# A fused linear-attention and gated-convolution kernel: a list scheduler in place of a hand-made order, with cheaper matmul work

## The chip, the cores and the metric

The kernel runs on one core of one Trainium2 chip. The metric is the device time of one execution in microseconds (us). A "span" is the time from the first to the last instruction in the profile; the time is 1.7 to 3.1 us longer in all runs with both on record.

The engines, as the profile calls them: PE is the matmul engine (PEld are its weight loads), DVE is VectorE, ACT is ScalarE, POOL is GpSimd, SP is SyncE, which here only issues DMAs. Each engine takes its own work in the order of the program: in the trace of the changed kernel, the 69 operations of POOL, 104 of DVE and 183 of ACT that could be matched by name all ran in the planned order.

## The reference, cut to what matters

The first stage is a recurrent attention over 4 batches x 8 heads x 768 steps x 48 channels; the second is a projection, a circular convolution through an FFT, a gate and an output projection on 4 x 768 x 384.

```python
for t in range(S):                                   # stage 1, per batch and head
    cur = einsum('bhd,bhe->bhde', u * k_t, v_t)
    y[:, :, t] = einsum('bhd,bhde->bhe', r_t, state + cur)
    state = w_t[..., None] * state + einsum('bhd,bhe->bhde', k_t, v_t)
# stage 2, x = y with heads joined
x1, x2, x3 = split(x @ w_proj, 3)
x2_conv = irfft(rfft(x2) * rfft(filter), n=S)        # along the sequence
out = (x1 * x2_conv * x3) @ w_out
```

Both kernels cut the sequence into chunks of 128 steps, so there are 24 chunks, 6 to a batch. In a chunk, cumulative sums of log(w) turn the recurrence into a masked 128 x 128 product of scaled q and k for each head, plus one product with the state. The FFT is a set of matmuls with a cosine/sine table `F`; the inverse uses its transpose `m2`.

## The kernel before: the parts that the change touches

The kernel before emits its instructions in an order made by hand: a loop over the chunks, with second-stage work dealt out between the steps of a chunk by a credit counter (`fill`). Chunk i+1's first steps are put between chunk i's scores and its output.

```python
for idx in range(len(chunks)):
    turn(idx); begin(idx + 2); load_weights(idx); issue_loads(idx + 4)
    fill(FILL[0])                        # up to n pieces of second-stage work
    ...
    scores(idx); decay(idx + 1); bonus_b(idx + 1); bonus_a(idx + 2)
    fill(FILL[1]); output(idx); fill(FILL[2]); turn_x(...); ...
```

A chunk's q is turned as fp32 and scaled after it (`qT = rT * e`); the scale itself is computed turned (`csT`):

```python
nc.tensor.matmul(csi, mask_incl, lg[:, :, 0:D], ...)
for j in range(HP):
    nc.tensor.matmul(csT[:, j, :], lg[:, 2*j:2*j+2, :], mask_incl, ...)
for j in range(HP):
    nc.tensor.transpose(rT[:, j, :], rb[:, 2*j:2*j+2, :], ident_f)      # fp32
...
nc.vector.tensor_mul(qT, rT, e[:, :, 0:L])
```

The POOL engine does four products and a cast per chunk, always: `rk`, `rku`, `vc` and `kh`, and the cast of `v`. The sums that the convolution needs read their second half from PSUM, where PE has just written it:

```python
nc.vector.tensor_add(z("sd0")[:, :, sl], lo, hi)     # lo in SBUF, hi = the PSUM tile yt
nc.vector.tensor_sub(z("sd1")[:, :, sl], lo, hi)
```

The inverse transform takes 36 matmuls of 128x384 per batch, 6 for each of 3 column blocks and 2 halves of the sequence:

```python
for q in range(6):
    m = m2n[:, q - 2, :] if (hf and q >= 2) else m2[:, q, :]
    nc.tensor.matmul(ps, z(f"P{q % 2}")[:, q // 2, cb*L:(cb+1)*L], m, start=(q == 0), stop=(q == 5))
nc.vector.tensor_mul(z("y")[:, cb, sl], ps, z("g")[:, cb, sl])
```

## Time and profile before

| | before |
|---|---|
| time, median of the first three runs | 197.75 us |
| span of the profiled run | 193.0 us |
| busy: PE / DVE / ACT / POOL | 82% / 73% / 57% / 61% |
| start of the first scores matmul | 15.06 us |
| batch period (start of the product P, batch to batch) | 38.6 and 40.2 us |
| PE's own work, counted start to start | 144.7 us |
| PE's idle time: 0-45 us / 45-163 us / rest | 24.3 / 17.8 / 6.2 us |

Matmuls overlap in the pipeline (one of 128x384 lasts 0.326 us, but the next starts after 0.163), so the busy time counts too much. I took the times from one matmul's start to the next one's start, capped each at about the usual value of its line and shape, and called the remainder idle. A stretch at a lower PE clock counts as idle this way too.

These lines are from the page of the kernel before: the span, the busy time of each engine, PE's busy tenths and its clock in 40 slices of the span, the DMA engines' busy tenths, and the engines' shares of the chain that ended last.

```profile
span 193.0 us, 4267 instructions
...
PE 157.3 (82%) x1538; PEld 103.8 (54%) x1538; DVE 140.8 (73%) x267; ACT 110.0 (57%) x233; POOL 117.5 (61%) x162
...
PE   0068677977949859999999599999998699999792
...
PEclk9999958999999999999999969999999999999999
DMA  6999999999999991987499929384950000042024
...
PE 66%; DVE 18%; issue 6%; ACT 5%; DMA 2%; POOL 2%; SPq 0%; ACTq 0%; DVEq 0%; POOLq 0%
```

PE is the busiest engine and 66% of the chain, but no engine is full. In the first slices PE is only partly busy while the DMA engines are nearly full: loads are the likely limit in the first 45 us, and the second stage has little work to give yet.

The view of waits shows the stalls of the fixed order. Each line says which engine and line waited for what, and then the total, the number of waits and the longest one, in us.

```profile
ACT en L322 <- PE csi L313: 25.6, 14, 4.9
PE sc L350 <- DVE tkT L338: 7.1, 8, 1.8
PE ps_i L487 <- DVE P_1801 L481: 2.5, 1, 2.5
PE ps_i L487 <- DVE P_2531 L481: 2.5, 1, 2.5
PE ps_i L487 <- DVE P_1071 L481: 2.5, 1, 2.5
```

PE waits 2.5 us before the inverse of three batches for DVE's product P, and 7.1 us in front of scores for a DVE copy.

### The profile page before, as it was taken

The page shows a single profiled execution, that of the slowest core. Times are in us where ns is not written, and L with a number is a line of the kernel's source. Part 1 is how long each engine was busy: PE and PEld are TensorE (multiplying, and loading weights), DVE is VectorE, ACT ScalarE, POOL GpSimd, SP SyncE. Part 2 cuts the span into 40 slices and gives each one's busy share as a digit, 9 for nine tenths or more (in the row PEclk, how much of TensorE's full clock was granted, in tenths as well). Part 3 has the DMA queues.
Part 4 walks back from the last instruction along what each step waited for, and adds up shares of the span by engine and source line. Part 5 has one row for each costly group of instructions (what it writes and reads, how often), then busy time and mean ns, then how long its engine had stood idle before and what let it go on. Part 6 is the DMA issues. An engine that isn't in the chain of part 4 may idle for free.

```text
span 193.0 us, 4267 instructions
## 1 busy us (share of the span) xinstructions
PE 157.3 (82%) x1538; PEld 103.8 (54%) x1538; DVE 140.8 (73%) x267; ACT 110.0 (57%) x233; POOL 117.5 (61%) x162
## 2 busy tenths in 40 slices
PE   0068677977949859999999599999998699999792
PEld 0047456655626526666666266676764466555350
DVE  7427865886688998977559976896669898608840
ACT  2954434577848642457987423479887224597023
POOL 5079887979865793868777936767797584000000
PEclk9999958999999999999999969999999999999999
DMA  6999999999999991987499929384950000042024
GB/s 124 180 201 180 198 196 198 293 185 196 183 173 183 188 169 27 166 156 128 140 242 188 169 47 163 74 148 83 297 100 3 0 2 3 0 161 89 0 77 168
DMA packets 104806, 26.43 MB, mean 137 GB/s; under 512 B 100049, under 2 KB 104401, under 8 KB 104785
## 3 DMA queue, kind: packets, MB, share of 16 engines
q1 hardware_dynamic: 103984, 24.98, 70.9%
q0 software_dynamic: 800, 1.18, 3.4%
q8 instruction: 12, 0.20, 0.5%
q14 instruction: 10, 0.07, 0.2%
HBM read 22.61 MB, written 4.72 MB: 142 GB/s over the span
## 4 chain that ended last, share of the span: by engine, by line
PE 66%; DVE 18%; issue 6%; ACT 5%; DMA 2%; POOL 2%; SPq 0%; ACTq 0%; DVEq 0%; POOLq 0%
PE ps_i L487 11%; PE ps_p L430 7%; PE rT L319 6%; PE ps_o L497 5%; PE sc L350 5%; PE ps_f L227 4%; PE csT L315 3%; PE yn L383 3%; PE ps_f L219 2%; DVE tkT L338 2%; PE csi L313 2%; PE kv L360 2%; PE kv L362 2%; PE yn L375 2%; PE yt L396 2%
## 5 line engine op out<-in xcount | busy, mean ns | idle before, releaser
L355 DVE TENSOR_TENSOR mt<-sc,mask_excl 128x1024 bf16<-128x1024 f32 x24 | 29.2, 1217 | 6.9 <-PE sc L350 6.9
L303 POOL TENSOR_TENSOR vc<-v,cc 128x384 bf16<-128x384 bf16 x24 | 21.0, 874 | 15.9 <-DVE cc L302 8.7
L322 ACT ACTIVATE en<-csi 128x384 f32<-128x384 f32 x24 | 11.9, 495 | 27.9 <-PE csi L313 25.6
L293 POOL TENSOR_TENSOR rku<-rk,u_bc 128x384 bf16<-128x384 bf16 x24 | 24.4, 1019 | 1.9
L324 POOL TENSOR_TENSOR kh_83<-ld_k,en 128x384 bf16<-128x384 f32 x12 | 12.0, 1002 | 20.6 <-ACT en L322 20.6
L492 DVE TENSOR_TENSOR y<-ps_i,g 128x384 bf16<-128x384 f32 x24 | 13.3, 556 | 8.6 <-PE ps_i L487 8.6
L388 ACT ACTIVATE xn<-yn 128x384 bf16<-128x384 f32 x24 | 11.8, 491 | 12.7 <-PE yn L383 11.7
L294 POOL CAST v<-ld_v 128x384 bf16<-128x384 f32 x24 | 16.6, 692 | 0.0
L501 ACT ACTIVATE o<-ps_o 128x384 f32<-128x384 f32 x24 | 11.1, 496 | 9.1 <-PE ps_o L497 9.1
L350 PE MATMUL sc<-qT,tkT 48*128 48x128 bf16 x192 | 10.0, 226 | 7.6 <-DVE tkT L338 7.1
L430 PEld LDWEIGHTS <-wproj 128*128 128x128 bf16 x144 | 12.5, 97 | 5.6 <-issue 0.3
L324 POOL TENSOR_TENSOR kh_84<-ld_k,en 128x384 bf16<-128x384 f32 x12 | 12.0, 1004 | 5.5 <-ACT en L322 5.4
L338 DVE COPY tkT<-tk 128x512 bf16<-128x512 bf16 x24 | 10.0, 418 | 6.8 <-PE tk L336 6.6
L302 DVE TENSOR_REDUCE cc<-rku 128x8 f32<-128x384 bf16 x24 | 13.0, 542 | 1.7 <-POOL rku L293 1.7
L497 PE MATMUL ps_o<-wout,y 128*128 128x384 bf16 x72 | 13.8, 326 | 0.0
L350 PEld LDWEIGHTS <-tkT 48*128 48x128 bf16 x192 | 5.6, 97 | 15.0 <-DVE tkT L338 12.5
L313 PE MATMUL csi<-lw_81,mask_incl 128*128 128x384 bf16 x12 | 4.3, 358 | 9.9 <-ACT lw_81 L280 9.9
L328 DVE TENSOR_TENSOR qT<-rT,e_85 128x512 bf16<-128x512 f32 x12 | 8.3, 688 | 5.2 <-PE rT L319 5.1
L367 DVE TENSOR_TENSOR S<-kv,phi 128x384 bf16<-128x384 f32 x20 | 10.9, 546 | 0.0
L396 PE MATMUL yt<-ident,xn 128*128 128x128 bf16 x72 | 8.3, 227 | 2.5 <-ACT xn L388 2.5
L227 PE MATMUL ps_f<-ab,F 128*128 128x384 bf16 x48 | 10.1, 327 | 0.0
L383 PE MATMUL yn<-v,mt 128*128 128x48 bf16 x192 | 9.1, 186 | 0.3 <-DVE mt L355 0.3
(256 smaller groups left out, 461.4 us busy)
## 6 DMA issues: line engine op xcount, KB each, us to landing
ld_w<-in_w_dram SPq DMA_DIRECT2D x24, 192.0 KB, 4.7
ld_k<-in_k_dram SPq DMA_DIRECT2D x24, 192.0 KB, 4.7
ld_v<-in_v_dram SPq DMA_DIRECT2D x24, 192.0 KB, 4.6
out_dram<-o SPq DMA_DIRECT2D x3, 1152.0 KB, 5.7
filt<-in_moe_filter_fft_dram SPq DMA_DIRECT2D x1, 1152.0 KB, 7.5
out_dram<-o SPq DMA_DIRECT2D x6, 192.0 KB, 1.9
r_76<-in_r_dram SPq DMA_DIRECT2D x5, 192.0 KB, 4.0
r_77<-in_r_dram SPq DMA_DIRECT2D x5, 192.0 KB, 4.8
```

The costliest lines, as they stand in the source:

```text
L227: nc.tensor.matmul(ps, F[:, ti, c0:c0 + L], x[:, ti, :], start=(ti == 0), stop=(ti == NT - 1),)
L293: nc.gpsimd.tensor_mul(t["rku"], rk, u_bc)
L294: nc.gpsimd.tensor_copy(out=t["vb"], in_=t["lv"])
L303: nc.gpsimd.tensor_mul(t["vc"], t["vb"], cc.to_broadcast([L, H, D]))
L324: nc.gpsimd.tensor_mul(kh[:, :, 0:D], t["lk"], en)
L338: nc.vector.tensor_copy(out=tkT, in_=tk)
L350: nc.tensor.matmul(sc[:, par, j, :], tkT[p0:p0 + D, j, :], qT[p0:p0 + D, j, :], start=True, stop=True,)
L355: nc.vector.tensor_mul(mt, sc.rearrange("p q j t -> p (q j) t"), _mid(mask_excl, H))
L383: nc.tensor.matmul(y[:, h, :], mt[:, HP * (h % 2) + h // 2, :], vb[:, h, :], start=False, stop=(h == H - 1),)
L430: nc.tensor.matmul(ps, wproj[:, cb, col0:col0 + L], xT[:, cb, sl], start=(cb == 0), stop=(cb == CB - 1),)
L487: nc.tensor.matmul(ps, z(f"P{q % 2}")[:, q // 2, cb * L:(cb + 1) * L], m, start=(q == 0), stop=(q == 5),)
L497: nc.tensor.matmul(ps, z("y")[:, cb, ti * L:(ti + 1) * L], wout[:, cb, :], start=(cb == 0), stop=(cb == CB - 1),)
```

## The change

Its intent: (1) every piece of work is declared as an operation with its inputs, outputs, candidate engines, assumed durations and a due time, and a list scheduler orders them for all engines, handing out PSUM banks as it goes; (2) q and k are both scaled in natural layout and turned together in bf16, so that the fp32 transposes and the turned sums go; (3) the state is kept per head, half as wide; (4) the inverse computes the even and odd parts over half the length, 18 matmul times for 36, and adds and subtracts them afterwards; (5) the sine tables are made during batch one and not at the start. The planner runs while the kernel is built, so the chip sees a fixed order again. The diff, cut to its core:

```diff
+SLACK = {PE: 0.073, ACT: 0.040, DVE: 0.000, POOL: 0.463, SP: 0.0}
+def pool(n, h=None): ...; return (POOL, h, h + 0.06, True)      # True: takes the shared port
+def dve2(n, lock=False): h = n/1920.0 + 0.069; return (DVE, h, h + 0.09, lock)
+    def order(self):
+        ...
+                    est = max(free[e], t0 + hop)
+                    if lock: est = max(est, port)
+        ...        # per engine: earliest est; within SLACK of it, the earliest due
+            if lock: port = est + hold
+            if o.bus:
+                start = est + hold + 1.1
+                dma = max(dma, start) + o.bus
+                o.end = 1.0 + (dma if e == SP else min(dma, start + 1.6 * o.bus))
...
+            op(f"ld_{name}{i}", T(i, -8 + 0.1 * n), [(SP, 0.06, 0.1, False)], ...load..., bus=0.98)
...
-        for j in range(HP):
-            nc.tensor.matmul(csT[:, j, :], lg[:, 2*j:2*j+2, :], mask_incl, ...)
-        for j in range(HP):
-            nc.tensor.transpose(rT[:, j, :], rb[:, 2*j:2*j+2, :], ident_f)
+        op(f"csx{i}", T(i, 0.7), [pe(C, 1, 1, 1, 1)], cx, ...)
+        op(f"kh{i}", T(i, 1.9), [pool(C), dve(C, True)], ...)      # POOL or DVE, as it falls
+        op(f"qh{i}", T(i, 2.0), [pool(C), dve(C, True)], ...)
+        op(f"tr{i}", T(i, 3.0), [pe(*[L] * 8)], tr, ...)           # k and q turned together
+        op(f"rk{i}", T(i, 1.5), [pool(C), dve(C, True)], ...)
+        op(f"rku{i}", T(i, 2.5), [dve2(C, True)], ...)             # was on POOL
...
-        sums(ci - NT, yt)                                   # second half from PSUM
+            hi = xT[bx][:, :, HALF + ti*L:HALF + (ti+1)*L]  # second half from SBUF
+                op(f"sd{b}.{q}.{ti}", d, [dve2(C, True)], ...)
...
-            for q in range(6): ... (for each half)
+            for q in (0, 1): matmul(pe_, P[q][:, 0, cs], m2[:, q, :], ...)
+            for q in (0, 1): matmul(po, P[q][:, 2, cs], m2[:, 4 + q, :], ...)
+            for q in (0, 1):
+                matmul(pe_, P[q][0:DP, 1, cs], m2[0:DP, 2 + q, :], ...)
+                matmul(po, P[q][DP:L, 1, cs], m2[DP:L, 2 + q, :], ...)
+            ev = copy(pe_); eo[0] = po + ev; eo[1] = ev - po; y = eo * g
```

The planner knows of the port that VectorE and GpSimd share (`lock`).

## The prediction

> **What bounds the kernel now.** Time 197.75 us, span 193.0. The chain of waits that ended last is 66% PE, 18% DVE. The page shows PE busy 82%, DVE 73%, ACT 57%, POOL 61%: no engine is full. PE's busy time includes pipeline overlap, so I counted start-to-start times in the timeline: a 128x384 matmul 0.163 us, an attention chunk about 2.4 us (rT 0.45, csT 0.22, tk 0.22, sc 0.33, kv 0.34, yn 0.53, yt 0.17, csi 0.16), a batch's second stage about 20.8 (inverse 36 x 0.163 = 5.9). That is 58 + 83 + 4.5 (tables, filter) = 146 us of 193. The chain in order of time shows a batch every 40.2 us (inverse at 111.15 and 151.37), PE's own work being 35. The rest is stalls of a fixed order: 2.5 us before each inverse for DVE's product P, PE before scores on tkT, ACT on csi (25.6 us in total), POOL on en; about 12 us start-up (first scores at 15.06, behind three Sins and a second table load); a tail of 30 us after the last chunk.
>
> **What the change does.**
> - PE: the half-length inverse takes 18 matmul times less per batch: -2.9 us each, -11.7. Chunk: fp32 rT (0.45) and csT (0.22) go; csx (0.16 plus four one-column sums, 0.1) and four more bf16 transposes (0.22) come; the state is half as wide: 2.2 us, -5 in all. New PE sum about 130.
> - DVE, start-to-start: mt 1.12, qk 0.60, cc 0.46, rku 0.27, state 0.27 (was 0.47): 2.7 us; qT (0.60) becomes an SBUF product for POOL or DVE. Second stage about 13 us per batch. With tables about 125 us, plus what it takes from POOL.
> - ACT: 0.37 us per 384: 2.0 per chunk, 10 per batch, tables 8.6: 100-115.
> - POOL: kh, qh, rk at 1.0, vc 0.83: at most 92-105, overflow to DVE.
> - Order: due times interleave all engines, so ready work fills the waits above. Sin tables leave the start: -6 us.
> - DMA: loads of 192 KB at about 196 GB/s, 1.0 us each; all traffic about 125 us: fits, not loosely.
>
> **Critical path.** PE (130) and DVE (125-135) become near-full. PE 130 + start-up 9 + idle while batch one has no second stage 8 + tail gaps 5 + stalls 2 = span about 154. The time was 2 to 5 us above the span: 158 us. Range 150 to 168. Faster by over 2%: 0.95; within 2%: 0.03; slower: 0.02.
>
> **The skill.** "SBUF — State Buffer" calls the port pair of VectorE and GpSimd an exclusive lock, taken also by a VectorE op with two SBUF inputs against GpSimd reads. The trace agrees: the 128x1152 product U takes 0.74 us, but 1.55 when POOL runs rk. rku, y, and any qh/kh/rk on DVE join this class: POOL's 92 us plus about 38 of DVE share one port. "VectorE: DVE Perf Modes", tier table, gives two-input ops 2x only on bf16 SBUF operands; sd's 0.27 agrees, so rku should take 0.27.
>
> **What would show it.** Right: batch period falls from 40.2 to 31-34; ps_i matmuls halve; PE's idle before the inverse largely gone; PE over 55% of the chain; first scores before 11 us; DVE busy over 80%.
>
> **What would make it wrong.** In-order queues whose static order drifts from the chip (late loads, port lock), so one late item blocks ready ones: 165+. PSUM: two y banks and two inverse banks of six. 48-column matmuls dearer than 25 ns. Or fewer stalls than I allow: 150.

## The result, and the profile after

| | before | after |
|---|---|---|
| time, median (range) | 197.88 (195.08-199.01) us, 4 runs | 180.96 (180.28-181.66) us, 4 runs |
| span of the profiled run | 193.0 us | 179.9 us |
| busy DVE / POOL | 140.8 / 117.5 us | 148.7 / 74.3 us |
| first scores matmul | 15.06 us | 9.61 us |
| batch period | 38.6, 40.2 us | 37.8, 36.2 us |
| PE's own work | 144.7 us | 133.9 us |
| PE idle: early / middle / tail | 24.3 / 17.8 / 6.2 us | 24.4 / 13.2 / 8.4 us |

The ratio of the fast runs is 0.921, with a 95% interval of 0.914 to 0.929. A ratio is the mean time of one kernel's fast runs over that of the other's fast runs of the same rounds, so it isn't quite the ratio of the medians. All four runs after were fast, and the output was correct. "Early" is 0 to 45 us, "tail" about the last 20 us (30 before), "middle" the rest.

So the change gained 17 us where 40 were predicted. The page after, in the same lines as before:

```profile
span 179.9 us, 4559 instructions
...
PE 149.2 (83%) x1698; PEld 90.5 (50%) x1698; DVE 148.7 (83%) x290; ACT 136.5 (76%) x304; POOL 74.3 (41%) x87
...
PE   0553988197999999998999988679999999998761
...
PEclk9999996569999999999999999969999999999998
DMA  5999999699999899999999984467000001500006
...
PE 49%; DVE 29%; DMA 9%; issue 7%; ACT 2%; POOL 2%; SPq 1%; DVEq 0%; POOLq 0%; ACTq 0%
```

Three things stand out. PE's share of the chain has fallen to 49%, and DVE's has risen to 29%: PE did not become the limit. DMA has 9% of the chain. And in slices 7 to 9 (about 27 to 40 us) PE's clock falls, and in slice 8 its busy digit too. The waits before the inverse, for comparison with those of before:

```profile
PE bank L675 <- DVE P L661: 1.3, 1, 1.3
PE bank L673 <- DVE P L661: 1.2, 2, 0.8
```

Those fell from three times 2.5 us to 2.5 us in all. That part of the intent worked.

The table of PE work says where the 13.1 us of span came from: 10.8 us less PE work and 2.3 us less idle time (48.3 to 46.0). (The time fell by 17 us, more than the span, because the profile after is of the slowest of its four runs, at 181.66 us, and the profile before of a fast one.) The new order filled 4.6 us of the middle's idle time, gave 2.2 back in the tail, and did nothing for the first 45 us.

### Two suspects in the trace

**The port.** These are the first groups of DVE and then of POOL in the timeline after, at the product of batch two: start, duration, engine, line, operation, operands and count. Both engines multiply SBUF operands without a pause ("x2" is two in a row).

```profile
101.91 1.09 DVE L661 TENSOR_TENSOR U<-X,HI 128x1152 bf16<-128x1152 bf16 x1
102.92 1.55 DVE L661 TENSOR_TENSOR U<-X,HG 128x1152 bf16<-128x1152 bf16 x1
104.39 3.02 DVE L661 TENSOR_TENSOR P<-U,U 128x1152 bf16<-128x1152 bf16 x2
101.39 1.00 POOL L278 TENSOR_TENSOR rk<-r,k 128x384 bf16<-128x384 f32 x1
102.34 1.52 POOL L278 TENSOR_TENSOR kh<-k,en 128x384 bf16<-128x384 f32 x1
103.81 1.52 POOL L278 TENSOR_TENSOR qh<-r,ep 128x384 bf16<-128x384 f32 x1
105.29 1.51 POOL L278 TENSOR_TENSOR kh<-k,en 128x384 bf16<-128x384 f32 x1
```

The two products P took 3.02 us, and kh and qh on POOL 1.5 us each, with nothing else in their way; POOL's rk, at the start, took 1.00. A P that meets no POOL work takes 0.75 us (an experiment below). Over the whole kernel I summed what each DVE instruction took over the shortest of its own form: 5.3 us before, 18.1 us after. The largest shares after are sd (3.2), P, rk and y (2.3 to 2.4 each) and rku (1.9).

The Trainium skill, page "SBUF — State Buffer", section "SBUF: two separate sides", calls this port pair an exclusive lock that one engine holds for a whole instruction while the other "fully blocks". The trace agrees: 4 DVE products from 101.91 to 107.4 us and the POOL products beside them took turns.

**The early loads.** The SP queue's timeline after, at the weights' loads (the filter on SP's queue; the projection weights, wproj, on POOL's queue at 21.2 us): start and duration of each issue.

```profile
20.40 0.70 SPq L549 DMA_DIRECT2D filt<-in_moe_filter_fft_dram  x1
21.22 1.19 SPq L349 DMA_DIRECT2D w<-in_w_dram  x1
22.52 1.72 SPq L349 DMA_DIRECT2D v<-in_v_dram  x1
24.33 4.18 SPq L349 DMA_DIRECT2D k<-in_k_dram  x1
28.60 5.78 SPq L349 DMA_DIRECT2D r<-in_r_dram  x1
34.47 0.58 SPq L349 DMA_DIRECT2D w<-in_w_dram  x1
```

An issue usually takes 0.7 us. Here two of them held SP for 4.18 and 5.78 us, and what was issued behind them started late. While SP was still held, from about 33 to 35 us, the DMA engines moved only 30 to 40 GB/s: they were not full all the time. The kernel before has such issues too (4.08 and 3.83 us), so this loss is not new. The median load takes 3.9 us from issue to landing; the w of chunk 5 took 13.3 us, and the r of chunk 5 was issued at 28.6 and landed at 36.8. POOL, which works in order, stood at chunk 5's rk for that r:

```profile
POOL rk L278 <- DMA r<-in_r_dram: 14.2, 4, 8.6
```

In the windows view, PE then had no work from 31 to 35 us. The columns are: window and its length, busy us and count for PE, PEld, DVE, ACT and POOL, the PE clock, the DMA engines' share, GB/s.

```profile
25.00:28.00 3.00, 1.88 (x43) 1.24 (x40) 2.94 (x4) 2.54 (x7) 2.76 (x3) 1.00 1.12 280
28.00:31.00 3.00, 2.91 (x40) 1.91 (x38) 3.00 (x8) 1.72 (x4) 0.29 (x1) 0.58 1.10 202
31.00:35.00 4.00, 0.00 (x1) 0.00 (x0) 2.97 (x5) 0.45 (x2) 0.00 (x0) 0.50 0.62 124
35.00:38.00 3.00, 2.88 (x14) 1.24 (x15) 0.36 (x1) 2.22 (x7) 0.99 (x1) 0.50 0.99 193
```

The clock is a loss of its own: it fell to half already at about 28.5 us, when PE was partly busy and its longest gap had been 0.85 us, and it stayed there to 38.8. Over the first 45 us it averaged 0.89 (0.92 before, with half clock from 23.9 to 30.7 us).

The product after the scores of chunk 5 started at 43.8 us, against 44.2 us before. The head start of 3 us at chunk 0 (12.6 against 15.7 us) was gone.

### The profile page after: what moved, and what is told of

Its sections match the earlier page's. It is cut to its first block, busy times and chain, and to the rows that moved or that the text cites. A ratio compares the mean times of both kernels' runs of the same rounds, so it can differ in the third digit from the quotient of the medians.

```text
span 179.9 us, 4559 instructions
## 1 busy us (share of the span) xinstructions
PE 149.2 (83%) x1698; PEld 90.5 (50%) x1698; DVE 148.7 (83%) x290; ACT 136.5 (76%) x304; POOL 74.3 (41%) x87
## 4 chain that ended last, share of the span: by engine, by line
PE 49%; DVE 29%; DMA 9%; issue 7%; ACT 2%; POOL 2%; SPq 1%; DVEq 0%; POOLq 0%; ACTq 0%
DMA r<-in_r_dram 9%; PE bank L594 9%; PE bank L630 7%; PE bank L703 5%; DVE mt L420 4%; DVE U L661 4%; PE bank L516 4%; DVE y L692 3%; PE bank L391 3%; PE sc L414 3%; PE bank L462 3%; DVE eo L689 2%; PE bank L448 2%; DVE P L661 2%; PE bank L509 2%
## 5 line engine op out<-in xcount | busy, mean ns | idle before, releaser
L594 PE MATMUL bank<-xT,wproj 128*128 128x384 bf16 x144 | 28.4, 326 | 0.0
L278 POOL TENSOR_TENSOR kh<-k,en 128x384 bf16<-128x384 f32 x16 | 18.4, 1150 | 23.1 <-ACT en L375 21.7
L278 POOL TENSOR_TENSOR vc<-vb,cc 128x384 bf16<-128x384 bf16 x15 | 12.7, 855 | 33.1 <-DVE cc L404 24.7
L278 POOL TENSOR_TENSOR rk<-r,k 128x384 bf16<-128x384 f32 x16 | 17.3, 1078 | 14.9 <-DMA r<-in_r_dram 14.2
L282 ACT ACTIVATE qk<-bank 128x1024 bf16<-128x1024 bf16 x20 | 20.7, 1033 | 2.5 <-PE bank L391 1.8
L278 POOL TENSOR_TENSOR qh<-r,ep 128x384 bf16<-128x384 f32 x17 | 19.5, 1149 | 3.9 <-ACT ep L378 3.9
L703 PE MATMUL bank<-wout,y 128*128 128x384 bf16 x72 | 14.7, 350 | 3.5 <-DVE y L692 3.4
L282 ACT ACTIVATE xn<-bank 128x192 bf16<-128x192 f32 x48 | 13.8, 344 | 4.1 <-PE bank L462 3.6
L594 PEld LDWEIGHTS <-wproj 128*128 128x128 bf16 x144 | 12.5, 97 | 7.0 <-issue 0.3
L630 PE MATMUL bank<-wproj,sd 128*128 128x384 bf16 x72 | 14.2, 326 | 0.9 <-DVE sd L621 0.9
L611 DVE TENSOR_TENSOR g<-bank,x 128x384 bf16<-128x384 f32 x24 | 12.7, 548 | 2.4 <-ACT ab L282 1.6
## 6 DMA issues: line engine op xcount, KB each, us to landing
wproj<-in_moe_w_proj_dram POOLq DMA_DIRECT2D x1, 864.0 KB, 13.1
```

What stands on the lines that cost most here:

```text
L278: (nc.vector if e == DVE else nc.gpsimd).tensor_mul(o, a, b)
L282: nc.scalar.activation(out=o, in_=a, func=AF.Copy)
L594: nc.tensor.matmul(p, wproj[:, cb, col0:col0 + L], xT[bx][:, cb, sl], start=(cb == 0), stop=(cb == CB - 1),)
L611: op("c" + n3, d + 0.3, [dve(C)], lambda e, bk: nc.vector.tensor_mul(g[bx][:, fb, sl], bank[bk[n3]][:, 0:HALF], x1[0][:, fb, sl]), r=[f"x1 ...
L630: nc.tensor.matmul(bank[bk[n]][:, 0:C], sd[q][:, cb, ti * L:(ti + 1) * L], wproj[:, cb, C:2 * C], start=(cb == 0), stop=(cb == CB - 1),)
L703: nc.tensor.matmul(bank[bk[n]][:, 0:C], y[cb][:, ti * L:(ti + 1) * L], wout[:, cb, :], start=(cb == 0), stop=(cb == CB - 1),)
```

## The experiments

To compare the chip with the planner I ran the planner of the changed kernel by itself. It books the end at 160.3 us; that is the plan's own sum of assumed durations and no measurement. What follows calls "lag" the start of a chunk's masked-scores product (mt) on the chip, less its start in the plan. In the changed kernel it is 2.1 us at chunk 4, 8.0 at chunk 5, 12.5 at chunk 14 and 21.2 at chunk 23.

The theories: **A**, the port lock, beyond what the plan books for it. **B**, the weights' bytes and the blocked issues in the first 45 us. **C**, the plan is poor in itself, whatever the chip does.

### Without the lock: e1_nolock and e6_nolock2

POOL's products become memsets of about the same length, which read nothing, and a product of four elements that keeps the dependences. Their outputs are wrong, which doesn't matter for the times.

```diff
-        (nc.vector if e == DVE else nc.gpsimd).tensor_mul(o, a, b)
+        if e == DVE: nc.vector.tensor_mul(o, a, b)
+        else:
+            nc.gpsimd.tensor_mul(o[:, 0:1, 0:4], a[:, 0:1, 0:4], b[:, 0:1, 0:4])
+            for _ in range(2): nc.gpsimd.memset(o[:, 1:H, :], 1e-7)     # e1: 0.01
+            nc.gpsimd.memset(o[:, 0:1, 4:D], 1e-7)
```

> The changed kernel, same order on every engine, but GpSimd's products read only a 4-element corner of their inputs (so the waits stay) and fill the rest with memsets of about the same length: wrong values on purpose. Theory A (VectorE and GpSimd block each other on their shared port, which cost 20 us of VectorE time): VectorE products return to 0.35 / 0.55 / 0.75 us, VectorE busy falls from 149 to about 130, time falls from 181 to 170-174. Rival (the lost time is early DMA and order; the lock fills slack): durations fall, time stays 178-181.

> As e1, GpSimd's products made from a corner and memsets of the same length, now with small fill values so that nothing overflows, for a profile in the fast state. Theory A: 173-176 us again, VectorE busy 133-137 instead of 149, sd 0.35 and rku 0.35 on average, and the lag behind the planner's own times no longer grows between chunks 8 and 16 (it grew by 9 us there).

e1 gave 175.2 us over its three fast runs, ratio 0.8955 (0.886 to 0.906). Its profiled run took 270.77 us, which I can't explain; its fill of 0.01 gave a relative error of 3e17, so I took 1e-7 for e6, and read only e6's profile. e6 gave 174.31 us, ratio 0.8875 (0.881 to 0.894), against 0.921 for the changed kernel: 6.6 us less. DVE's sum of lengthening fell from 18.1 to 2.9 us, its busy time from 148.7 to 134.6, and POOL's busy time hardly moved (74.3 to 73.5). Between chunks 8 and 16 the lag grew by 2.3 us and not by 9.0. These groups (line, engine, operation, operands and shapes, count; busy us and mean ns; idle before) are first from the changed kernel and then from e6:

```profile
L621 DVE TENSOR_TENSOR sd<-xT 128x384 bf16<-128x384 bf16 x24 | 10.7, 474 | 2.6 <-ACT xT L282 2.4
L692 DVE TENSOR_TENSOR y<-eo,g 128x768 bf16<-128x768 bf16 x12 | 8.4, 739 | 0.0
L661 DVE TENSOR_TENSOR P<-U,U 128x1152 bf16<-128x1152 bf16 x6 | 6.7, 1148 | 0.0
L688 DVE TENSOR_TENSOR eo<-bank,ev 128x384 bf16<-128x384 f32 x12 | 6.6, 551 | 1.7 <-ACT ev L282 1.7
```

```profile
L627 DVE TENSOR_TENSOR sd<-xT 128x384 bf16<-128x384 bf16 x24 | 7.7, 350 | 2.8 <-ACT xT L288 2.7
L698 DVE TENSOR_TENSOR y<-eo,g 128x768 bf16<-128x768 bf16 x12 | 6.1, 551 | 0.0
L667 DVE TENSOR_TENSOR P<-U,U 128x1152 bf16<-128x1152 bf16 x6 | 4.3, 750 | 0.0
L694 DVE TENSOR_TENSOR eo<-bank,ev 128x384 bf16<-128x384 f32 x12 | 6.7, 554 | 2.1 <-ACT ev L288 1.9
```

sd went from 474 to 350 ns, y from 739 to 551 and P from 1148 to 750, while the sum eo, one of whose inputs is in PSUM, stayed at about 552. That is what the same section of the skill's SBUF page says: a VectorE operation with two SBUF inputs is held up only by a GpSimd operation that reads SBUF.

The batch periods of e6 were 34.4 and 32.7 us, and PE had 70% of the chain:

```profile
PE 70%; DMA 10%; DVE 9%; ACT 5%; issue 2%; POOL 1%; SPq 1%; ACTq 0%; POOLq 0%; DVEq 0%
```

So the 31 to 34 us that I had predicted is about what this order gives where nothing takes the port. Theory A holds, for part of the loss: the lag at chunk 23 was 13.3 us, not zero, and its step at chunk 5 was still there (0.9 to 6.5 us).

### The weights' bytes: e2_light, e3_both and e12_light2

```diff
-            out=wproj, in_=moe_w_proj.rearrange("(n p) f -> p n f", p=L)), ...
+            out=wproj[:, 0:1, 0:C], in_=moe_w_proj.rearrange(...)[:, 0:1, 0:C]), ...      # 1/9
-            out=filt, in_=moe_filter_fft.rearrange("(n p) c -> p n c", p=L)), ...
+            out=filt[:, 0:1, :], in_=moe_filter_fft.rearrange(...)[:, 0:1, :]), ...       # 1/6
```

> The changed kernel, same order, but the loads of the projection weights and of the filter move a ninth and a sixth of their bytes (the rest is memset at the start on GpSimd, wrong values on purpose). Theory B (these two loads delay chunk 5's r by 6 us while the pipeline has nothing else, and the delay is never recovered): chunk 5's r lands near 31 instead of 36.8, first scores product of chunk 5 at 37-38 instead of 43.8, time 173-176. Rival (VectorE is the limit, so an early start is lost again by the third batch): time 178-181.

> Both edits together. If A and B are separate causes they add: about 163-168 us, near the end of 160 us that the kernel's own planner sets down for its order. If one hides behind the other, the time is that of the better one alone (170-174).

These two were my mistake. To leave no part of the tiles unwritten I had put two memsets into the start on POOL, and the memset of the filter tile then waited 19.47 us for that tile's load. The kernel stood still for 17 us in its first chunks: 193.97 us (ratio 0.995) and, with the lock taken away, 187.71 us (0.960). They say nothing of theory B. e12 does it without memsets; instead each reader takes the small part that was loaded.

> The changed kernel, same order; the loads of projection weights and filter move a ninth and a sixth of the bytes, and their readers use the small part (wrong values on purpose; e2 done rightly). Early DMA volume as the cause of the 6 us lag at chunk 5: r of chunk 5 lands at 27-30 instead of 36.8, chunk 5's scores product at 37-39 instead of 43.8, time 174-177. If VectorE takes it back later: 179-181.

e12 gave 178.13 us, ratio 0.915 (0.905 to 0.925): 2.8 us less by the medians, 1.3 by the ratios, so the size is loose; it lies between the two ranges expected. In the profile the step is plain. The r of chunk 5 landed at 28.2 and not 36.8 us, the lag at chunk 5 was 3.8 and not 8.0 us, but at chunk 23 it was 17.7 of 21.2. The issues that had been held, of k and r of chunk 5, were short again:

```profile
22.63 1.45 SPq L349 DMA_DIRECT2D k<-in_k_dram  x1
24.18 1.06 SPq L349 DMA_DIRECT2D r<-in_r_dram  x1
```

So it is the bytes that held them. The gain is small beside the scatter: a second profile of the unchanged kernel (e14, below) had lags of 5.9 and 19.9 us where the first had 8.0 and 21.2. Theory B holds for some 2 to 3.5 us.

### A later load of wproj: e5_late and e7_late_nolock

```diff
         for est, o, e, bk in plan.order():
+            if o.name == "wproj": held = o; continue
+            if o.name == "rk5": held.fn(POOL, {})        # issue it just ahead of rk5 on POOL
             o.fn(e, bk)
```

> The changed kernel with right results and the same order everywhere, but the issue of the projection weights' load moves on GpSimd's queue from after kh of chunk 2 (21.2 us) to just before rk of chunk 5, about 28 us. Theory B (this load shares the DMA engines with chunk 5's loads, which then take 8 to 13 us each instead of 4): chunk 5's r lands at 30-32 instead of 36.8, its scores product is at 38-40 instead of 43.8, and the 4-5 us stay to the end: 175-177 us. Rival (VectorE is the limit and gives it back): 179-181.

> Both: if the two causes are separate, the gains add: about 168-171 us. If they overlap: 173-176.

e5 gave 183.87 us, but three of its four runs were slow, at a clock of 0.83 in the profiled one, so it has no ratio; its one fast run took 179.93. e7: 176.73 us, ratio 0.898, against e6's 0.888, so 2.4 us worse, and above both ranges expected. In e7 the r of chunk 5 landed at 31.8 us, but chunk 6's product started at 52.0 us, later than the 49.8 of e6. The later load only moved the gap. In e7 SP was held for 4.06 us at 22.96 us, before wproj was issued at 29.69, with the filter alone on its way, and again for 4.52 us at 31.77. A likely reason is that the bytes have to go somewhere and the chunks' own loads already fill the DMA engines; no run shows it.

### Was it the planner's model, or its rule? e8_replan and e11_due

e8 tells the planner what the loads cost (0.70 us an issue, no load more than 3 us ahead of the bus) and takes the constants that then give the shortest plan, 164.7 us.

```diff
-                    ... [(SP, 0.06, 0.1, False)] ...
+                    if o.bus and e == SP: est = max(est, dma - BACK)          # BACK = 3.0
+                    ... [(SP, 0.70, 0.7, False)] ...
-PACE = 5.021; S2OFF, S2SPAN = 12.934, 29.153; TAB, FIL = 16.286, 20.392
+PACE = 5.703; S2OFF, S2SPAN = 21.321, 24.696; TAB, FIL = 22.154, 39.264
```

> The changed kernel with right results, its planner told what the trace shows of DMA: issuing a load takes 0.7 us of SyncE, no load is issued more than 3 us ahead of the DMA queue, the filter waits for Ln of chunk 5; its constants searched again for this. The planner's own end is 164.7 us (160.3 before, 169.0 for the old constants under the new DMA model). If the DMA model was what made plan and chip part, the lag at chunk 5 is about 2 us instead of 8 and the time 170-175 us; if the port lock alone counts, 178-183.

e8 was correct and took 186.24 us, ratio 0.948: slower than the changed kernel, and outside both ranges expected. It had more lock, 23.0 us of lengthening, and a lag at the end of 22.6 us. A better model of the loads alone did not bring the chip nearer to the plan.

e11 tests the rule itself: each engine takes the ready operation that is due first, even if it can't start yet.

```diff
-SLACK = {PE: 0.073, ACT: 0.040, DVE: 0.000, POOL: 0.463, SP: 0.0}
+SLACK = {PE: 1e9, ACT: 1e9, DVE: 1e9, POOL: 1e9, SP: 0.0}
```

> The changed kernel with right results, its planner always taking the work with the earliest due time on each engine instead of the one that can start earliest. Shows what the earliest-start rule is worth: planner's end 195.9 us, so 205-220 us on the chip, slower than the kernel before; if the due times alone do the interleaving, 180-186.

e11 took 218.77 us, ratio 1.121, with PE idle for some 83 us in all (with caps from the changed kernel), nearly twice as long. These are two runs, and the constants were not searched again for the other rule. So, with these constants, it is the rule of the earliest start that makes the order good, and the due times only break near ties.

### The cheaper inverse in the old order: e4_before_half

The kernel before with nothing but the inverse over half the length (the core of its edit is the last part of the change's diff above), put where the old inverse stood.

> The kernel before with only the half-length inverse (18 matmul times of 0.163 us less per batch, 11.7 us in all; VectorE gains 1.4 us of work per batch). If PE's work sets the time of the fixed order, 186-190 us, that is most of the whole change's gain; if the stalls around the inverse (product P before it) set it, 193-198 us.

The result was correct, and 214.9 us, where the kernel before took 195.66 in the same rounds: far outside both ranges, though PE's work had fallen by about 9 us (counted with the caps of the kernel before). Three of its four runs are slow, as over 1.5% above the fastest; the one fast run took 210.78 us, against 194.05 to 196.57 for the fast runs before, so the sign isn't in doubt. Its waits, in the same view as before:

```profile
PE sc L341 <- DVE tkT L329: 21.8, 13, 4.2
ACT ev L487 <- PE ps_d L484: 13.8, 12, 4.6
```

The wait of PE on tkT grew from 7.1 to 21.8 us. That fits the order: the additional ev and eo stand on ACT and DVE in front of the copies that the next chunk needs. But the lock may have a share: the gate product now reads SBUF twice beside a busy POOL, and DVE's lengthening was 10.4 us against 5.3. No run parts the two. PE was idle for about 78 us in all, against 46.0 in the changed kernel. This bears on what the scheduler was worth: the table of before and after shows only 2.3 us less idle, but this cheaper work, put where the old inverse stood, added idle time in the old order. Another place for it was not tried.

### The sums from PSUM, and a retuned plan: e9_sdpsum and e10_tuned

e9 gives the sums back their operand in PSUM, as in the kernel before. That takes them out of the lock: sd takes 343 ns on average and not 474.

```diff
-            hi = xT[bx][:, :, HALF + ti * L:HALF + (ti + 1) * L]
+            yt = f"yt{NCH * b + NT + ti}"
-                op(f"sd...", d, [dve2(C, True)], ... fn(sd[q][:, :, sl], lo, hi), r=[xT lo, xT hi], ...)
+                op(f"sd...", d, [dve2(C)], ... fn(sd[q][:, :, sl], lo, bank[bk[yt]] as bf16), r=[xT lo], uses=[yt])
```

> The changed kernel with right results; only the 24 sums and differences sd read the second half of xT from PSUM (the transposed tile itself, as the kernel before did) instead of from SBUF, so that they have one SBUF input and need not wait for GpSimd. Theory A (port lock): sd takes 0.35 us on average instead of 0.47, and with the waits of the first products behind them gone the time falls to 175-178 us. Rival: the products in question wait in slack, 180-182 us; or the PSUM bank held longer costs more, above 182.

e9 was correct and took 178.29 us, ratio 0.915 (0.903 to 0.927), a little above the range expected. It isn't a test of the operand alone: the planner, told that sd takes no lock, made a new order, in which some 25 operations changed their engine. DVE's lengthening fell only from 18.1 to 16.2 us, for qh grew where sd fell. e10 is e9 with e8's model of the loads and with constants searched on a replay of the fixed order that has the lock and the load queue in it (the replay said 169 to 170 us).

> As e9, with the planner told of the DMA queue as in e8, the filter after Ln of chunk 6, and its constants searched again, each order judged not by the planner's own end but by a replay in which the port lock goes to whoever comes first, loads queue as the trace shows, and durations vary by 8%. Replay: 169-170 us (the changed kernel in the same replay: 184-185, e8: 180-184). If lock and load queue are what makes plan and chip part, the time is 167-173 us, and better than both kernels; if something else, 176 or more.

e10 was correct and took 177.85 us, ratio 0.909 (0.898 to 0.920), above the 167 to 173 us expected. It had the least lock of the correct versions (13.7 us, in a profile marked slow), but at 28 us ACT stood at the next chunk's logarithm, whose w came late, beside wproj, and everything behind it in ACT's queue waited too:

```profile
33.23 0.52 ACT L360 ACTIVATE lg<-w 128x384 bf16<-128x384 f32 x1 [5.17 <-DMA w<-in_w_dram]
```

PE was idle for 5.03 us there, its clock fell to half 2.8 us into the gap, and the next matmuls ran at a clock of 0.50. The skill's page "TensorE: Matmul & The Clock Gate", section "What's actually happening", puts the fall to half rate after an idle window of about 3.4 us; this gap agrees only roughly, for the 3.4 us before the fall still held 0.6 us of matmuls. The fall at 28.5 us in the changed kernel came without such a gap.

### Do the two causes add up, and is the gain real? e13 to e16

Still open were whether A and B are separate losses, and whether e9 and e10 really beat the changed kernel, for their intervals overlapped with its own. e13 is e6 and e12 together; e14 is the changed kernel again, e15 is e9 and e16 is e10, all four on one chip, five rounds each (e13: three).

> The changed kernel with the lock-free multiplies on POOL and the small weight loads both (wrong result on purpose). Alone, the first gave 174.31 us and the second 178.13, against 180.96 for the changed kernel: 6.65 and 2.83 us less. If they are separate losses, they add: 171.5 us, and the lag of the last scores product behind the planner's own time falls from 21.2 to about 10. If both take away the same wait (the first chunks' late start), about 174 us, no better than without the lock. If everything that parts the chip from the plan (160.3 us) were these two, about 163 us.

> The changed kernel unchanged, once more, as the yardstick on this chip: 181 us, ratio to before 0.921 within 0.007. Nothing else is asked of it.

> The sums' second half read from PSUM. If the port lock on these six additions per batch is a real loss, 2 to 3 us below the run of the changed kernel of this call (178.3 against 181). If the earlier difference was chance, within 0.7 us of it.

> The same plus the planner told of the loads' real cost and its constants searched again. Before: 177.85 us. If the search on a replay with lock and load queue brought something beyond the PSUM edit, it is at least 1 us below that run of this call; if the replay only fitted its own model, it is equal to it.

| run | time | ratio to before (95%) |
|---|---|---|
| before, same rounds | 196.43 us | |
| e14, the changed kernel | 180.36 us | 0.917 (0.913-0.921) |
| e15, sums from PSUM | 177.78 us | 0.903 (0.899-0.906) |
| e16, and retuned | 178.17 us | 0.904 (0.899-0.908) |
| e13, no lock and light weights (wrong) | 169.60 us | 0.860 (0.855-0.865) |

e15 is the version to keep: correct, and faster than both kernels, by 2.6 us than the changed one, with intervals that don't touch. Retuning brought nothing beyond it: the replay had fitted its own model. e15 has the new order of e9 too, so the 2.6 us belong to both. e13 is 10.8 us below e14, where the two parts alone had given 6.6 and 2.8 by the medians (6.7 and 1.3 by the ratios): together they give at least their sum. Its page:

```profile
span 168.1 us, 4749 instructions
...
PEclk9999997599999999999999999999999999999998
...
PE 72%; DVE 12%; ACT 6%; POOL 5%; issue 3%; POOLq 0%; ACTq 0%; DVEq 0%
```

PE has 72% of the chain, and the short loss of clock at slices 7 and 8 is what is left of the early gap. The table of PE's idle time shows best that the two causes are separate ones:

| | span | PE work | idle, first 45 us | idle, middle | idle, tail |
|---|---|---|---|---|---|
| before | 193.0 | 144.7 | 24.3 | 17.8 | 6.2 |
| after | 179.9 | 133.9 | 24.4 | 13.2 | 8.4 |
| light weights (e12) | 176.4 | 134.2 | 20.8 | 13.1 | 8.3 |
| no lock (e6) | 171.9 | 133.6 | 23.3 | 6.6 | 8.5 |
| both (e13) | 168.1 | 133.8 | 19.4 | 6.5 | 8.4 |
| predicted | 154 | 130 | 17 | 2 | 5 |

The weights act in the first 45 us and nowhere else, the lock acts in the middle and hardly elsewhere, and neither touches the tail. (In the second profile of the changed kernel, e14, the idle time of the first 45 us is 1.4 us shorter than in "after" and the rest the same, by the 75th percentile as cap; so the weights' part is 2 to 3.6 us. The limits of "middle" and "tail" were moved with each kernel's last chunk.)

## Why the prediction was wrong, point by point

The direction was right, the size was not: 158 us predicted, 150 to 168 as the range, 180.96 measured. The prediction's sum was "PE 130 + start-up 9 + idle while batch one has no second stage 8 + tail gaps 5 + stalls 2 = span about 154". Set against the trace, the 25.9 us between 154 and 179.9 split as follows. (The time is 1.8 us above the span, where the prediction allowed 4, so luck hid 2 us of this.)

1. **"stalls 2" was 13.2 us.** This is the step that failed most, by 11.2 us. The prediction named the lock, quoted a product U that took 1.55 us and not 0.74, and even added up that POOL's 92 us and about 38 us of DVE share one port. But the sum on the critical path then booked nothing for it. e6 shows what it cost: 6.6 us of the 13.2 went with the lock, and the batch period fell to 34.4 and 32.7 us, where the prediction had 31 to 34 and the changed kernel has 37.8 and 36.2. The other 4.6 us over the 2 remain without the lock and without the weights' bytes, and stay open.
2. **Start-up and batch one, "9" and "8", were 24.4 us together**, 7.4 too few. The prediction said of the loads "fits, not loosely", from an average over the kernel. In the first 45 us the DMA engines are nearly full at about 200 GB/s, and the filter (1152 KB) and wproj (864 KB) have to pass in the same time. e12 takes their bytes away and wins back 3.6 us of idle time (3.9 without the lock; about 2 against e14). The rest stays open. First scores came at 9.61 us, before 11 as predicted, but nothing of this head start was left at chunk 5.
3. **"PE 130" was 133.9 us.** This level depends on the cap (129.8 us with the 75th percentile, and the stalls are then 16.0), the fall less so. PE's work fell by 10.8 us where 16 were expected (146 to 130). Of the two terms, the inverse gave 9.7 and not 11.7 (23.8 to 14.1 by its lines), and the chunk's lines gave 2.4 and not 5 (56.9 to 54.5): the state's products cost as much as before (6.2 us), and the pair of half-width products with vc more than the single one (6.2 us against 3.9).
4. **"tail gaps 5" were 8.4 us**, and no experiment changed that.

What it said would show each step right: ps_i's matmuls fell from 144 to 96 instructions, of which 48 run pairwise: half the matmul times, as said, though the measured time fell only to 59% (23.8 to 14.1 us). PE's idle time before the inverse is largely gone (8.3 us with the last batch's, to 2.5), as said. DVE is over 80% busy (83%), as said, but for another reason: some 15 of its 148.7 us are lengthening by the lock (18.1 with it, 2.9 without). "PE over 55% of the chain" was wrong at 49%, and it is the sign of the failed step: without the lock it is 70%. The batch period was wrong, see point 1.

The section on what would make it wrong named the mechanism: "in-order queues whose static order drifts from the chip (late loads, port lock)", and "165+". That mechanism was named rightly, but no term of the sum held it and its chance was set too low.

From the skill, "VectorE: DVE Perf Modes", section "The perf-mode tier table", has two-input products on bf16 in SBUF at twice the rate; rku took 349 ns without the lock, where the fp32 product kh of the same shape took 544. That agrees once the fixed part is taken off: rku and P (750 ns for three times the elements) give 0.52 ns an element and 148 ns fixed, which leaves 1.03 ns an element for kh. The table's single rate for a PSUM operand does not hold here: sd in the kernel before reads one bf16 operand from PSUM and took 344 to 355 ns, as fast as with both in SBUF (350 ns in e6). The 0.27 us of the prediction for rku was a start-to-start time; with the lock it was 417 ns long on average.

Theory C has a share too: the planner itself books 160.3 us for the span, 6 more than the 154 that I had summed up, so a chip that kept to the plan would still have missed the prediction's middle.

What stays open: with both causes taken away the span was 168.1 us against the plan's 160.3, and the lag grows slowly, from 0.6 us at chunk 4 to 2.5 at chunk 5, 5.7 at chunk 16 and 9.4 at chunk 23. I have not found what that is made of. Also, e13's POOL work reads less, so it may have removed a little more than the lock. The outlier of 270.77 us in e1 is unexplained.

## What to carry to other kernels

When work moves from one engine to another, book it on the resource that they share and not only on the engine: here 43 us of work left POOL, and a part of it came back as 15 us of waiting that no group's idle column shows, only its mean duration. Before moving a product to VectorE, see whether one of its inputs can still be read from PSUM; here that, with the new order that the planner made of it, gave 2.6 us. And check the load of the bus in the stretch where the constants arrive, not as an average: a static order has one late load block everything behind it in each in-order queue.

## What the Trainium skill lacked or had wrong

- "SBUF — State Buffer" tells of the lock but gives no durations for two engines that both work from SBUF without a pause (it quotes slowdowns of 6.8x and 1.5x for the two orders of issue). Here a DVE product of 0.75 us and a POOL product of 1.0 us each took about 1.5 us for as long as both went on, and about 15 us of DVE time were lost to it in a kernel of 180 us.
- "DMA: Bandwidth & Descriptors", section "Issuing engines are not separate DMA queues", says that the DMAs of all engines interleave on the same 16 DMA engines, which the trace agrees with (between 15 and 45 us SP's queue and POOL's took 82% and 15% of the 16 engines' time), and that what an issue costs the sequencer is usually small. It has no figure for an issue on SP while the DMA engines are full: here 4.18 and 5.78 us, where 0.7 is usual.
- The same page, section "Queues, rings and completion order", says that a DMA engine takes turns between queues packet by packet. It doesn't say what follows for small packets. Between 15 and 45 us, by the trace's count of packets, POOL's queue moved 0.88 MB in 400 packets (2.2 KB each) and SP's 5.25 MB in 22276 (236 bytes each), and loads on SP issued meanwhile landed after up to 13.3 us where 3.9 is usual. That the turns are the cause is an inference; no run here shows it.
- "TensorE: Matmul & The Clock Gate" ties the fall to half clock to an idle window. In the changed kernel it fell at about 28.5 us after three microseconds in which PE was busy for 1.88 us, in groups of small matmuls with no gap over 0.85 us, and stayed at half for 10 us. The page has no figure for how busy PE must be to keep its clock.
- "VectorE: DVE Perf Modes", section "The perf-mode tier table", gives two-input products the single rate for any operand in PSUM; sd, with one bf16 operand there, ran at the double rate (344 to 355 ns, see above).
